# SwiGLU feed-forward block: the order in which the first 512 rows of x are loaded, transposed and projected

## The chip, the cores and the metric

The kernel runs on one core of a Trainium2 chip. A core has a matrix engine (TensorE, here PE, whose weight loads are listed apart as PEld), a vector engine (VectorE, DVE), a scalar engine (ScalarE, ACT), GpSimd (POOL) and a sync engine (SyncE, SP); 16 DMA engines move data between the chip's memory and the core's on-chip memory (SBUF). Matmul results go to a small accumulator memory (PSUM). SP and ACT each have a queue on which they issue DMAs. The metric is the device time of one execution in microseconds.

## The reference

```python
B, S, D, F = 1, 2048, 640, 1536          # all in bfloat16
g = silu(x @ w_gate)                      # x [2048, 640], w_gate [640, 1536]
u = x @ w_up                              # w_up [640, 1536]
return (g * u) @ w_down                   # w_down [1536, 640]
```

## The kernel before, in words

The 2048 rows are worked in four blocks of 512 (`sb`). A block is four chunks of 128 rows. The contraction of the first two products runs over D = 640, five slices of 128 (`KD`); F = 1536 is twelve slices of 128 (`KF`, index `fc`).

For each block and each `fc`, `proj` makes five matmuls of 512 columns with the slices of `w_gate` as weights, into the PSUM tile `pg`, and five with `w_up`, into `pu` (line 134). ACT takes the Silu of `pg` (line 180), DVE multiplies it with `pu` into `aT` (line 181). After the twelve `fc` come the matmuls of the down projection (lines 189 and 213), whose results are copied and stored.

The matmuls need x transposed, with D across partitions (`xT`). For blocks 1 to 3 a transposing DMA brings it (line 97). For block 0 it would come too late, so its four chunks are loaded as they are into `x_sb`, TensorE transposes each with five 128x128 matmuls against an identity into a PSUM tile `pt` (line 125), and DVE or ACT copies `pt` into `xT` (line 130). The PSUM tiles `po_a` and `po_b`, two buffers each, serve for `pt`.

What sets the order at the front:

- Two queues, SP and ACT, take the first loads (lines 82 to 87): chunk 0 on SP and chunk 2 on ACT, then chunk 1 on SP and chunk 3 on ACT; then the first 128 columns of `w_gate`, three slices on SP and two on ACT, and the same of `w_up`. Then SP alone issues the rest: columns 128 to 384 of `w_gate` and of `w_up` (`W_CHUNKS[1]`), and the larger pieces after them (line 71), `w_down` (line 94), the transposing loads (line 97). ACT has a load of its function table and a Silu on one column (`silu_first`, line 89) after its four loads.
- Each engine works through its instructions in the order written. Loads get their completion semaphores from a set of eight in turn; a load that takes a semaphore for the second time is issued only when the load that used it last has landed. ACT's and SP's early loads alternate in this: in the kernel before, x takes four of the eight and the first columns of the weights the other four, so the first load of line 71 is the ninth and waits for chunk 2, and the next ones wait for chunks 0, 3 and 1.
- `keep_order` ties the instructions of TensorE and of ACT at the front to the order as written. `warm(n)` puts n matmuls of 128 columns on a tile of ones into TensorE's stream (line 103); nobody reads their result.
- TensorE's order is: 18 such matmuls, the transposes of chunk 0 and chunk 2, four more (`N_GAP`), the transposes of chunks 1 and 3, two more, then `proj_pair` twice: five matmuls (line 149) on chunks 0 and 2, 256 columns that lie in two groups of 128, and five on chunks 1 and 3; then `pu` with 512 columns, and so on.

Chunks 0 and 2 are copied by DVE, five slices at once. Of chunks 1 and 3 ACT copies the first two slices and DVE the other three.

Of the kernel before, what the change touches and what calls it, by code (L numbers as in the profile page):

```python
# [10 lines left out]
def _body(  # L11
# [8 lines left out]
    nc = tc.nc  # L20
    P = nc.NUM_PARTITIONS
# [11 lines left out]
    KD = D // P  # L33
    KF = F // P
    S_BLK = 512
# [1 line left out]
    SUB = S_BLK // P  # L37
    DA = 512
    Q = 32
    N_WARM, N_GAP = 18, 4  # L40
    W_CHUNKS = [(0, 1), (1, 3), (3, 6), (6, 9), (9, 12)]
    assert D % P == 0 and F % P == 0 and S % S_BLK == 0 and D > DA and SUB == 4

# [8 lines left out]
    x_sb = consts.tile([P, SUB, D], bf16)  # L52
    xT = consts.tile([P, KD, S], bf16)
    wg_sb = consts.tile([P, KD, F], bf16)
    wu_sb = consts.tile([P, KD, F], bf16)
# [5 lines left out]
    x_v = x2.rearrange("(c p) d -> p c d", p=P)  # L61
    xt_v = x2.rearrange("s (kd p) -> s kd p", p=P)
    wg_v = w_gate.rearrange("(kd p) f -> p kd f", p=P)
    wu_v = w_up.rearrange("(kd p) f -> p kd f", p=P)
    wd_v = w_down.rearrange("(kf p) d -> p kf d", p=P)

    def wslice(a, b):
        return slice(a * P, b * P)

    def load_w(eng, dst, src, a, b):  # L70
        eng.dma_start(out=dst[:, :, wslice(a, b)], in_=src[:, :, wslice(a, b)])

    def load_x(eng, c0, c1):
        eng.dma_start(out=x_sb[:, c0:c1, :], in_=x_v[:, c0:c1, :])

    ones = consts.tile([P, P], bf16)
    silu_first = consts.tile([P, 1], f32)
# [1 line left out]

    queues = (nc.sync, nc.scalar)  # L80
    halves = ((0, KD // 2 + 1), (KD // 2 + 1, KD))
    for c in (0, 1):
        for i, eng in enumerate(queues):
            load_x(eng, c + 2 * i, c + 2 * i + 1)
    for dst, src in ((wg_sb, wg_v), (wu_sb, wu_v)):
        for eng, (k0, k1) in zip(queues, halves):
            eng.dma_start(out=dst[:, k0:k1, wslice(0, 1)], in_=src[:, k0:k1, wslice(0, 1)])
    load_w(nc.sync, wg_sb, wg_v, *W_CHUNKS[1])
    nc.scalar.activation(silu_first[:], ones[:, 0:1], ACT.Silu)  # L89
    load_w(nc.sync, wu_sb, wu_v, *W_CHUNKS[1])  # L90
# [10 lines left out]
    def warm(n):  # L101
        for _ in range(n):
            nc.tensor.matmul(  # L103
                pw[:, 0:P], lhsT=ones[:], rhs=ones[:], start=True, stop=True
            )

    def keep_order(engine):

        traced = [i for i in nc.cur_bb.bb.instructions if i.engine == engine]
        for a, b in zip(traced, traced[1:]):  # L110
            tc.add_manual_dep(
                b,
                a.name,
                mybir.DependencyInfo(
                    mybir.DependencyClass.NoSync, mybir.DependencyReason.DATA
                ),
                reason="keep_order",
            )

    def transpose_chunk(c, parts):  # L120
        c_sl = slice(c * P, (c + 1) * P)
        for copy, tag, k0, k1 in parts:
            pt = psum.tile([P, k1 - k0, P], bf16, tag=tag, name="pt")
            for kd in range(k0, k1):
                nc.tensor.transpose(  # L125
                    out=pt[:, kd - k0, :],
                    in_=x_sb[:, c, kd * P : (kd + 1) * P],
                    identity=ident[:],
                )
            copy(out=xT[:, k0:k1, c_sl], in_=pt[:])  # L130

    def proj(ps, w_sb, fc, sb, c0, c1):
        for kd in range(KD):
            nc.tensor.matmul(  # L134
                ps[:, c0:c1],
                lhsT=w_sb[:, kd, fc * P : (fc + 1) * P],
                rhs=xT[:, kd, sb * S_BLK + c0 : sb * S_BLK + c1],
                start=(kd == 0),
                stop=(kd == KD - 1),
            )  # L140

    def proj_pair(ps, w_sb, fc, sb, b):


        def pair(ap):
            return ap.rearrange("p (a b c) -> p b a c", b=2, c=P)[:, b]

        for kd in range(KD):
            nc.tensor.matmul(  # L149
                pair(ps[:]),  # L150
                lhsT=w_sb[:, kd, fc * P : (fc + 1) * P],
                rhs=pair(xT[:, kd, sb * S_BLK : (sb + 1) * S_BLK]),
                start=(kd == 0),
                stop=(kd == KD - 1),
            )

    for sb in range(NSB):
        s_sl = slice(sb * S_BLK, (sb + 1) * S_BLK)
        for fc in range(KF):
            pg = psum.tile([P, S_BLK], f32, tag="gu", name="pg", bufs=4)  # L160
            pu = psum.tile([P, S_BLK], f32, tag="gu", name="pu", bufs=4)
            if sb == 0 and fc == 0:
                dve, act = nc.vector.tensor_copy, nc.scalar.copy
                warm(N_WARM)
                transpose_chunk(0, [(dve, "po_a", 0, KD)])
                transpose_chunk(2, [(dve, "po_b", 0, KD)])
                warm(N_GAP)
                for c in (1, 3):
                    transpose_chunk(c, [(act, "po_a", 0, 2), (dve, "po_b", 2, KD)])
                warm(2)  # L170
                proj_pair(pg, wg_sb, fc, sb, 0)
                proj_pair(pg, wg_sb, fc, sb, 1)
                proj(pu, wu_sb, fc, sb, 0, S_BLK)
                keep_order(mybir.EngineType.PE)
                keep_order(mybir.EngineType.Activation)
            else:
                proj(pg, wg_sb, fc, sb, 0, S_BLK)
                proj(pu, wu_sb, fc, sb, 0, S_BLK)
            sg = work.tile([P, S_BLK], f32)
            nc.scalar.activation(sg[:], pg[:], ACT.Silu)  # L180
            nc.vector.tensor_tensor(  # L181
                out=aT[:, fc, s_sl], in0=sg[:], in1=pu[:], op=ALU.mult
            )


        n_t = (SUB if sb < NSB - 1 else SUB - 1) * P
        po_t = psum.tile([P, n_t], f32, tag="po_b", name="po_t")
        for kf in range(KF):
            nc.tensor.matmul(  # L189
                po_t[:],  # L190
                lhsT=wd_sb[:, kf, DA:D],
                rhs=aT[:, kf, sb * S_BLK : sb * S_BLK + n_t],
                start=(kf == 0),
                stop=(kf == KF - 1),
            )
        ot_t = outp.tile([P, n_t], bf16, name="ot_t")
        ot_q = outp.tile([P, n_t], bf16, name="ot_q")
        nc.scalar.copy(ot_t[:], po_t[:])  # L198
        nc.vector.transpose(out=ot_q[:], in_=ot_t[:])  # L199
        for q in range(P // Q):  # L200
            nc.scalar.dma_start(
                out=out2[
                    sb * S_BLK : sb * S_BLK + n_t, DA + q * Q : DA + (q + 1) * Q
                ].rearrange("(i r) c -> r i c", r=Q),
                in_=ot_q[q * Q : (q + 1) * Q, :].rearrange("r (i c) -> r i c", c=Q),
            )

        for j in range(SUB):
            s0 = sb * S_BLK + j * P
            last = sb == NSB - 1 and j == SUB - 1  # L210
            po_a = psum.tile([P, DA], f32, tag="po_a", name="po_a")
            for kf in range(KF):
                nc.tensor.matmul(  # L213
                    po_a[:],
                    lhsT=aT[:, kf, s0 : s0 + P],
                    rhs=wd_sb[:, kf, 0:DA],
                    start=(kf == 0),
                    stop=(kf == KF - 1),
                )
            ot = outp.tile([P, DA], bf16, name="ot")  # L220
            nc.scalar.copy(ot[:], po_a[:])  # L221
            nc.sync.dma_start(out=out2[s0 : s0 + P, 0:DA], in_=ot[:])
            if last:
                po_b = psum.tile([P, D - DA], f32, tag="po_b", name="po_b")
                for kf in range(KF):
                    nc.tensor.matmul(  # L226
                        po_b[:],
                        lhsT=aT[:, kf, s0 : s0 + P],
                        rhs=wd_sb[:, kf, DA:D],
                        start=(kf == 0),  # L230
                        stop=(kf == KF - 1),
                    )
                ot_b = outp.tile([P, D - DA], bf16, name="ot_b")
                nc.vector.tensor_copy(out=ot_b[:], in_=po_b[:])  # L234
                nc.scalar.dma_start(out=out2[s0 : s0 + P, DA:D], in_=ot_b[:])
# [76 lines left out]
def kernel(tc, *args):  # L312
    _body(tc, *args)
    tc.close()
    tc.compile()
    _trim(tc.nc)
# [30 lines left out]
```

## Time and profile before

| what | value |
|---|---|
| median of six runs | 164.5 us (164.08 to 164.87) |
| the profiled execution's own time | 164.87 us |
| its span in the profile | 163.6 us |
| TensorE busy | 160.0 us, 98% of the span |
| weight loads (PEld) busy | 76.2 us, 47% |
| DVE busy | 37.8 us, 23% |
| ACT busy | 42.5 us, 26% |
| granted TensorE clock | 1.00 of full |

All times inside the profile count from the start of the span, which is SP's first DMA issue. In the timeline a line gives the start, the time, the engine, the line of the kernel, the operation, the tiles it writes and reads, and how many were merged; in brackets stands how long the engine had been idle before and what ended it. SPq and ACTq are the DMA issues on the queues of SP and ACT. In the list of DMA issues, the last number is the time from the issue to the landing. A matmul's record overlaps with the next one's, so the distance of their starts is the pace, not their duration.

### The profile page before, as it was taken

The numbers are of one execution on the slowest core, as the hardware profiler recorded it, in microseconds if no ns is written. First come the engines' busy times: TensorE is split into PE (matmuls) and PEld (weight loads), VectorE is DVE, ScalarE is ACT, GpSimd is POOL, SyncE is SP. The second block draws the span as 40 slices with busy tenths as digits, with TensorE's granted clock in tenths as the row PEclk, the third lists the DMA queues.
The fourth block names the chain that finished last, engine by engine and source line by source line (L and its number), as shares of the span: only waits on it lengthen the run. The fifth ranks groups of instructions, "written<-read, shape, count | busy, mean of one in ns | idle before, by whom it ended". The sixth has DMA issues, their size and how long they took to land.

```text
span 163.6 us, 1869 instructions
## 1 busy us (share of the span) xinstructions
PE 160.0 (98%) x766; PEld 76.2 (47%) x781; DVE 37.8 (23%) x58; ACT 42.5 (26%) x72; POOL 0.6 (0%) x6
## 2 busy tenths in 40 slices
PE   8999999999999999999999999999999999999994
PEld 7744444444444444444444444444444444445442
DVE  1233333310013333311003333331001333332000
ACT  3322222212142222212222222221214222222121
POOL 1000000000000000000000000000000000000000
DMA  7999999914100000003110000000420000000312
GB/s 217 272 334 329 364 125 220 204 23 68 64 32 0 0 0 0 4 0 34 64 64 0 2 4 0 0 0 0 64 68 32 0 0 0 0 0 4 53 35 72
DMA packets 26888, 11.26 MB, mean 69 GB/s; under 512 B 17664, under 2 KB 26880, under 8 KB 26880
## 3 DMA queue, kind: packets, MB, share of 16 engines
q1 hardware_dynamic: 17968, 10.16, 24.2%
q10 hardware_dynamic: 8912, 0.98, 3.9%
q8 instruction: 6, 0.10, 0.2%
q14 instruction: 2, 0.02, 0.0%
HBM read 6.55 MB, written 2.62 MB: 56 GB/s over the span
## 4 chain that ended last, share of the span: by engine, by line
PE 97%; DMA 2%; issue 1%; DVE 0%
PE pu L134 31%; PE pg L134 31%; PE po_a L213 25%; PE po_t L189 6%; DMA x_sb<-in_x_dram 2%; PE pt L125 1%; PE pg L149 1%; PE po_b L226 0%; PE pw L103 0%; DVE ot_b L234 0%
## 5 line engine op out<-in xcount | busy, mean ns | idle before, releaser
L134 PE MATMUL pu<-xT,wu_sb 128*128 128x512 bf16 x230 | 59.0, 379 | 0.5
L134 PE MATMUL pg<-xT,wg_sb 128*128 128x512 bf16 x235 | 58.4, 379 | 0.0
L181 DVE TENSOR_TENSOR aT<-sg,pu 128x512 bf16<-128x512 f32 x48 | 33.0, 687 | 100.9 <-PE pu L134 100.9
L180 ACT ACTIVATE sg<-pg 128x512 f32<-128x512 f32 x48 | 28.7, 597 | 71.6 <-PE pg L134 70.1
L213 PE MATMUL po_a<-wd_sb,aT 128*128 128x512 bf16 x188 | 41.9, 379 | 0.2
L134 PEld LDWEIGHTS <-wu_sb 128*128 128x128 bf16 x240 | 23.4, 98 | 28.2 <-DMA wu_sb<-in_w_up_dram 0.4
L134 PEld LDWEIGHTS <-wg_sb 128*128 128x128 bf16 x235 | 22.9, 98 | 27.9 <-DMA wg_sb<-in_w_gate_dram 0.4
L213 PEld LDWEIGHTS <-aT 128*128 128x128 bf16 x192 | 18.8, 98 | 22.6
L221 ACT CAST ot<-po_a 128x512 bf16<-128x512 f32 x16 | 9.4, 585 | 32.4 <-PE po_a L213 19.3
L189 PE MATMUL po_t<-aT,wd_sb 128*128 128x512 bf16 (+1 forms) x47 | 10.3, 365 | 0.1
L189 PEld LDWEIGHTS <-wd_sb 128*128 128x128 bf16 x48 | 4.7, 98 | 5.1
L198 ACT CAST ot_t<-po_t 128x512 bf16<-128x512 f32 (+1 forms) x4 | 2.2, 559 | 11.6 <-PE po_t L189 11.6
L199 DVE STREAM_TRANSPOSE ot_q<-ot_t 128x512 bf16<-128x512 bf16 (+1 forms) x4 | 2.7, 678 | 9.1 <-ACT ot_t L198 9.1
L103 PE MATMUL pw<-ones 128*128 128x128 bf16 x24 | 3.2, 313 | 0.4 <-DVE ones L78 0.4
L103 PEld LDWEIGHTS <-ones 128*128 128x128 bf16 x24 | 2.6, 148 | 0.4 <-DVE ones L78 0.4
L125 PE MATMUL pt<-ident,x_sb 128*128 128x128 bf16 x20 | 2.5, 313 | 0.2 <-DMA x_sb<-in_x_dram 0.2
L234 DVE CAST ot_b<-po_b 128x128 bf16<-128x128 f32 x1 | 0.3, 291 | 9.9 <-PE po_b L226 9.9
L130 DVE COPY xT<-pt 128x640 bf16<-128x640 bf16 (+1 forms) x4 | 1.7, 424 | 3.8 <-PE pt L125 3.8
L125 PEld LDWEIGHTS <-x_sb 128*128 128x128 bf16 x20 | 2.1, 147 | 0.5 <-DMA x_sb<-in_x_dram 0.5
L89 ACT ACT_TABLE_LOAD x1 | 1.3, 1283 | 2.0 <-issue 2.0
L149 PE MATMUL pg<-xT,wg_sb 128*128 128x256 bf16 x10 | 1.5, 310 | 0.0
L149 PEld LDWEIGHTS <-wg_sb 128*128 128x128 bf16 x10 | 1.1, 119 | 0.2
(11 smaller groups left out, 3.6 us busy)
## 6 DMA issues: line engine op xcount, KB each, us to landing
out_dram<-ot SPq DMA_DIRECT2D x16, 128.0 KB, 1.7
wd_sb<-in_w_down_dram SPq DMA_DIRECT2D x1, 1920.0 KB, 12.9
wg_sb<-in_w_gate_dram SPq DMA_DIRECT2D x3, 480.0 KB, 7.7
wu_sb<-in_w_up_dram SPq DMA_DIRECT2D x3, 480.0 KB, 7.5
out_dram<-ot_q ACTq DMA_DIRECT2D x12, 32.0 KB, 1.9
x_sb<-in_x_dram SPq DMA_DIRECT2D x2, 160.0 KB, 2.9
x_sb<-in_x_dram ACTq DMA_DIRECT2D x2, 160.0 KB, 3.3
wg_sb<-in_w_gate_dram SPq DMA_DIRECT2D x1, 320.0 KB, 4.8
```

The source lines that it names most:

```text
L103: nc.tensor.matmul(pw[:, 0:P], lhsT=ones[:], rhs=ones[:], start=True, stop=True)
L125: nc.tensor.transpose(out=pt[:, kd - k0, :], in_=x_sb[:, c, kd * P : (kd + 1) * P], identity=ident[:],)
L130: copy(out=xT[:, k0:k1, c_sl], in_=pt[:])
L134: nc.tensor.matmul(ps[:, c0:c1], lhsT=w_sb[:, kd, fc * P : (fc + 1) * P], rhs=xT[:, kd, sb * S_BLK + c0 : sb * S_BLK + c1], start=(kd == 0 ...
L149: nc.tensor.matmul(pair(ps[:]), lhsT=w_sb[:, kd, fc * P : (fc + 1) * P], rhs=pair(xT[:, kd, sb * S_BLK : (sb + 1) * S_BLK]), start=(kd == ...
L180: nc.scalar.activation(sg[:], pg[:], ACT.Silu)
L181: nc.vector.tensor_tensor(out=aT[:, fc, s_sl], in0=sg[:], in1=pu[:], op=ALU.mult)
L189: nc.tensor.matmul(po_t[:], lhsT=wd_sb[:, kf, DA:D], rhs=aT[:, kf, sb * S_BLK : sb * S_BLK + n_t], start=(kf == 0), stop=(kf == KF - 1),)
L198: nc.scalar.copy(ot_t[:], po_t[:])
L199: nc.vector.transpose(out=ot_q[:], in_=ot_t[:])
L213: nc.tensor.matmul(po_a[:], lhsT=aT[:, kf, s0 : s0 + P], rhs=wd_sb[:, kf, 0:DA], start=(kf == 0), stop=(kf == KF - 1),)
L221: nc.scalar.copy(ot[:], po_a[:])
```

## The change

Chunks 0 and 1 are each loaded in two halves of 64 rows, one half on each queue; after them chunk 2 goes on SP and chunk 3 on ACT. That makes three x loads on each queue in place of two. The loads of the weights follow in the same order as before. With two loads more ahead of line 71, the semaphores are met one load earlier on each queue: the first loads of `w_up` take those of the two halves of chunk 0, the first two loads of line 71 those of the halves of chunk 1, and the next two those of chunks 3 and 2.

TensorE transposes the chunks in the order 0, 1, 2, 3, with three fillers in place of four between the second and the third. Chunk 2's copy becomes one DVE copy of five slices; chunk 3's stays shared by ACT and DVE. The first gate projection works on columns 0 to 256 and then on 256 to 512, which are now contiguous, so `proj_pair` goes. The tiles `po_a` and `po_b` of the transposes are shared out anew.

```diff
-    N_WARM, N_GAP = 18, 4
+    N_WARM, N_GAP = 18, 3
...
-    def load_x(eng, c0, c1):
-        eng.dma_start(out=x_sb[:, c0:c1, :], in_=x_v[:, c0:c1, :])
+    def load_x(eng, c, p0, p1):
+        eng.dma_start(out=x_sb[p0:p1, c, :], in_=x_v[p0:p1, c, :])
...
+    def load_halves(dst, src, a, b):
+        for eng, (k0, k1) in zip(queues, halves):
+            eng.dma_start(out=dst[:, k0:k1, wslice(a, b)], in_=src[:, k0:k1, wslice(a, b)])
+
     for c in (0, 1):
         for i, eng in enumerate(queues):
-            load_x(eng, c + 2 * i, c + 2 * i + 1)
-    for dst, src in ((wg_sb, wg_v), (wu_sb, wu_v)):
-        for eng, (k0, k1) in zip(queues, halves):
-            eng.dma_start(out=dst[:, k0:k1, wslice(0, 1)], in_=src[:, k0:k1, wslice(0, 1)])
+            load_x(eng, c, i * P // 2, (i + 1) * P // 2)
+    for i, eng in enumerate(queues):
+        load_x(eng, 2 + i, 0, P)
+    load_halves(wg_sb, wg_v, *W_CHUNKS[0])
+    load_halves(wu_sb, wu_v, *W_CHUNKS[0])
...
                 transpose_chunk(0, [(dve, "po_a", 0, KD)])
-                transpose_chunk(2, [(dve, "po_b", 0, KD)])
+                transpose_chunk(1, [(dve, "po_b", 0, KD)])
                 warm(N_GAP)
-                for c in (1, 3):
-                    transpose_chunk(c, [(act, "po_a", 0, 2), (dve, "po_b", 2, KD)])
+                transpose_chunk(2, [(dve, "po_a", 0, KD)])
+                transpose_chunk(3, [(act, "po_b", 0, 2), (dve, "po_a", 2, KD)])
                 warm(2)
-                proj_pair(pg, wg_sb, fc, sb, 0)
-                proj_pair(pg, wg_sb, fc, sb, 1)
+                proj(pg, wg_sb, fc, sb, 0, 2 * P)
+                proj(pg, wg_sb, fc, sb, 2 * P, S_BLK)
                 proj(pu, wu_sb, fc, sb, 0, S_BLK)
```

More of the change, by code (lines that the diff above doesn't have):

```diff
@@ L140, in proj @@
             )
[L142 to L155, printed above, removed]
     for sb in range(NSB):
```

## The prediction

> **What bounds the kernel now.** The page comes first: how much of the span is tensor work, and what the chain that ended last is made of.
>
> ```profile
> span 163.6 us, 1869 instructions
> ...
> PE 97%; DMA 2%; issue 1%; DVE 0%
> ```
>
> TensorE is the chain nearly from end to end; nothing in the steady part is changed, so the edit can move only the 2% of DMA and the 1% of issue at the front. The chain cut to the first 12 us shows where these lie.
>
> ```profile
> 0.00 2.67 DMA x_sb<-in_x_dram
> 2.67 0.05 issue
> 2.71 1.25 PE pt L125 x10
> 3.96 0.43 PE pw L103 x4
> 4.38 1.07 PE pt L125 x10
> 5.45 0.21 PE pw L103 x2
> 5.67 1.33 PE pg L149 x10
> 7.00 0.05 issue
> 7.05 1.03 PE pu L134 x4
> ```
>
> The first load of x lands at 2.67, and from then on TensorE is never without work: ten transposes, four fillers, ten transposes, two fillers, the first gate projection. That picture suggests that an earlier first chunk is worth its full gain. The timeline of all engines says otherwise:
>
> ```profile
> 0.40 2.10 PE L103 MATMUL pw<-ones 128*128 128x128 bf16 x18 [0.40 <-DVE ones L78]
> ...
> 2.05 1.28 ACT L89 ACT_TABLE_LOAD   x1 [2.05 <-issue]
> 2.71 0.98 PEld L125 LDWEIGHTS <-x_sb 128*128 128x128 bf16 x10 [0.48 <-DMA x_sb<-in_x_dram]
> ...
> 3.08 0.37 SPq L71 DMA_DIRECT2D wg_sb<-in_w_gate_dram  x1
> ...
> 7.96 0.76 PEld L134 LDWEIGHTS <-wg_sb 128*128 128x128 bf16 x5 [0.38 <-DMA wg_sb<-in_w_gate_dram]
> ...
> 9.07 0.76 PEld L134 LDWEIGHTS <-wu_sb 128*128 128x128 bf16 x5 [0.35 <-DMA wu_sb<-in_w_up_dram]
> ```
>
> A weight load (PEld) waits at 7.96 for the second chunk of w_gate and at 9.07 for that of w_up. Both come just as TensorE needs them: the pu block before (five at the 0.215 us pace of the later blocks, the first missing from the records) began at about 6.84 and was through at 7.91, so TensorE itself lost some 0.05 us. After 9.08 the blocks follow every 1.08 us without a wait. So the end is set by the later of two things: TensorE's own work up to 7.91, and the arrival of these two loads. The list of DMA issues gives their price:
>
> ```profile
> wg_sb<-in_w_gate_dram SPq DMA_DIRECT2D x1, 320.0 KB, 4.8
> wu_sb<-in_w_up_dram SPq DMA_DIRECT2D x1, 320.0 KB, 5.5
> ```
>
> 3.08 + 4.8 = 7.9 and 3.49 + 5.5 = 9.0. SP issues the first as late as 3.08 because it waits: 1.2 us, by the waits of SP, for a load of x. The loads take turns on eight completion semaphores, and the ninth load must see its semaphore's first load, x chunk 2 on ACT (issued 0.12, landed 2.9 later), come in.
>
> **Change, part by part.** (Landing = issue + time to landing, from the x tile's own view: SP's loads 2.7 and 3.0 us, ACT's 2.9 and 3.6, issued at 0.00, 0.45, 0.12 and 0.57.) The four chunks landed at about 2.67 (chunk 0), 3.02 (2), 3.5 (1) and 4.13 (3), one after the other.
>
> *Chunk 0 in halves.* Bytes and order stay: first 160 KB, then 160 KB, and so on, over the same 16 engines. What could come earlier is the ramp: in 1.0 to 1.6 us only 60 packets moved, at 128 GB/s, all on SP's queue; in 1.6 to 2.4 it was 346 GB/s with both. Bounds for the start of the first transpose, now 2.71: down to 2.29, the end of the 18 fillers (last start 2.18 plus 0.107), and up by 0.22, if the first half of chunk 1 slips in ahead of ACT's half (80 KB at the 359 GB/s of the stretch 2.4 to 3.2). *Chunk 1 next.* It takes the place that chunk 2 had, 3.02; transposes of a chunk take 5 x 0.107 = 0.53. Second block: before 3.24, now no earlier than 3.02. So at most 0.22 of the 0.42 survives.
>
> The Trainium skill ("DMA: Bandwidth & Descriptors", Rules for kernel authors) speaks against this edit: of two transfers to disjoint partition halves it says "Don't bother — they serialize", since both use the same engines. By that rule the first transpose stays at 2.71, and the filler alone would be saved. The one-queue ramp speaks a little for the edit, and no row here decides.
>
> *N_GAP 4 to 3.* One filler, 0.107 us, leaves TensorE's stream. *Chunks 2 and 3.* Wanted at 3.02 + 0.53 + 0.32 = 3.87 and 4.41 at the earliest; they have the third and fourth places, 3.5 and 4.13, so nothing waits. TensorE's own stream thus becomes 0.11 to 0.33 us shorter (longer by 0.11 in the bad case); I take 0.2, between.
>
> *Copies.* Chunk 2's copy is one on DVE (0.49) where ACT (0.37) and DVE (0.36) shared it. A copy starts 0.75 after its chunk's first transpose (2.71 to 3.46): chunk 3's last ends by 4.41 + 0.75 + 0.36 = 5.52; the second half of the projection, which reads it, comes five matmuls of 0.21 after 5.13, at 6.2. Covered by 0.7. *Projection.* Ten 128x256 matmuls remain; their pace, 0.21 and later 0.109, is half of that of 512 columns, so the strided pairing cost nothing that could be saved.
>
> *One more DMA on each queue* (0.43 us each on SP by the gate load's row, 0.46 on ACT). The first w_gate loads move from 0.91 to about 1.36 and from 1.04 to 1.5. They landed at 4.75 and 4.98; at worst 0.45 later, 5.2, against a need at 5.46 - 0.33 = 5.13: at most 0.07, and likelier nothing, since their bytes stand behind all of x, 640 KB, which at these rates moves until 3.2 or so.
>
> *New wait.* There are ten loads before the big ones, for eight semaphores: the first w_up load on each queue now waits for its half of chunk 0. Queued behind it on ACT: table load and the warm Silu, 2.02 us from that issue to their end (1.53 to 3.55); with chunk 0 at 2.29 to 2.67 they end at 4.31 to 4.69, before ACT's copy is wanted (0.45 after its chunk's first transpose, as 4.63 after 4.18, so 4.86 and later). Cover 0.2, then another 0.7 of the copy's own. On SP: w_up's issue (0.49), then the second w_gate chunk, which also waits for ACT's half of chunk 1. So it goes out at the later of 2.67 + 0.49 + 0.05 = 3.2 and 3.02 + 0.06 = 3.08. Bounds: 2.83 (chunk 0 at 2.29, chunk 1 at chunk 0's old 2.67) and 3.5 (ACT's half of chunk 1 takes 2.9 from its issue at 0.57): 0.25 earlier to 0.42 later than 3.08. I take 3.14, 0.06 later, between the two nearest. First w_up itself: 2.67 + 4.0 = 6.67 at worst, needed at 6.5 to 6.7; not counted.
>
> *Sum.* TensorE reaches its need of w_gate at 7.91 - 0.2 = 7.7; the load lands at 7.9 + 0.06. The load decides: the gain turns into a longer wait at 7.96, and the end moves by +0.06. The profiled execution took 164.87 (163.6 of span and 1.27 around it), so 164.93; it stands 0.37 above the median of the runs, 164.5, so on their scale about 164.6. A change of 0.3%, 0.5 us, is about what a measurement of this kernel can tell.
>
> The trace has one more thing that could spoil the sum. The granted clock reads 1.00 throughout, yet the first three 128x256 matmuls take 421 to 348 ns and those from 6.07 on 272: the pace doubles there. The skill ("TensorE: Matmul & The Clock Gate", Part 1) says that this follows about 3.4 us of activity, counted by a window that does not start with the kernel. By that page the step may move between runs; an estimate from it, 1 us later, would cost 0.5 us, of which the longer wait would now absorb 0.2.
>
> **Rivals.**
> *The weights do not bind (faster).* If in most executions they land 0.3 us earlier than in this profile, TensorE's own stream counts in full: 0.33 at the best ordering, with the 0.05 stall 0.38; should chunk 1 come early too, 0.42 + 0.11 + 0.05 = 0.58. Time 163.9 to 164.2. For it: the profiled execution is the slowest of those shown (164.08 to 164.87). Against: both 0.38 and 0.35 waits stand in it.
> *The weight stream slips by a whole issue (slower).* One DMA more per queue delays the second w_gate and w_up chunks by 0.42 to 0.49: 165.0. Place: SP before the line 71 loads; it decides as soon as they go out after 3.2. For it: the rate of the DMA dips to 147 GB/s in 4.4 to 5.2, just where these loads start, so what is issued later is not caught up. Against: SP idled 1.2 us there.
> *ACT late (slower).* The table load behind a late chunk 0 would have to slip by 0.9 us before TensorE waits; at 3.2 instead of 2.67, it costs nothing yet. Price past that one for one, 0.3: 164.9.
> *Halving does nothing.* Chunk 0 lands at 2.67 as before: TensorE gains only 0.11, and the weights decide as in the forecast: 164.6.
>
> **How the numbers follow.** Weights decide, with or without an earlier chunk 0: 0.55 (within 0.3% 0.46, slower 0.06, faster 0.03). Weights not binding: 0.18 (faster 0.14, the rest within). Whole issue: 0.22 (slower 0.17). ACT: 0.05, slower. So faster 0.17, same 0.55, slower 0.28. Range: the likeliest case from 0.25 earlier to 0.42 later is 164.25 to 164.9; the rivals take it to 163.9 and 165.2 (0.49 on top of up to 0.2 of drift between medians).
>
> **What would show it.** Right: the wait of the weight load for w_gate before about 7.96 grows from 0.38 to 0.5 or more while the first transpose or the projection is earlier; the line 71 loads go out between 3.0 and 3.3; SP's and ACT's first w_up issue stand behind chunk 0's landing. Wrong: no wait for w_gate and a block at 9.08 moved earlier (first rival), line 71 at 3.4 or later (second), or TensorE waiting for xT.

## The result and the profile after

The changed kernel is slower: 166.03 us in the median of 21 runs (164.81 to 166.91) against 164.48 in 45 runs of before (163.87 to 164.89), a ratio of 1.0090 with an interval of 1.0075 to 1.0105. In two later sets of runs it took 165.58 against 164.24 (1.0072, 1.0036 to 1.0108) and 165.38 against 164.43 (1.0066, 1.0038 to 1.0094). Not only the median rose: the runs of before lie within 1.0 us, those of the changed kernel within 2.1. One more run of it, at 167.61, lies over 1.5% above its fastest; it counts as slow and is left out.

The profiled execution of the changed kernel took 165.41, near the low end of its runs, while that of before, 164.87, stood at the high end of its own. So these two profiles show only 0.5 us of the 1.5. First the page of the changed kernel:

```profile
span 164.1 us, 1870 instructions
...
PE 96%; DMA 2%; issue 1%; ACTq 0%; DVE 0%
```

The chain of the first 12 us (start, length, what) says where the 0.5 us came in. The second half of chunk 1, issued by ACT at 0.70, now stands in it in place of chunk 0:

```profile
0.12 0.54 ACTq L74
0.66 0.04 issue
0.70 3.04 DMA x_sb<-in_x_dram
3.73 0.05 issue
3.78 0.71 PE pt L131 x5
4.49 0.32 PE pw L109 x3
4.81 1.07 PE pt L131 x10
```

The timeline of the changed kernel, with the idle time before an instruction and what ended it in brackets:

```profile
0.00 1.83 SPq L74 DMA_DIRECT2D x_sb<-in_x_dram  x3
0.12 2.00 ACTq L74 DMA_DIRECT2D x_sb<-in_x_dram  x3
...
2.68 0.45 PEld L131 LDWEIGHTS <-x_sb 128*128 128x128 bf16 x5 [0.46 <-DMA x_sb<-in_x_dram]
...
3.75 0.37 SPq L71 DMA_DIRECT2D wg_sb<-in_w_gate_dram  x1
3.77 0.45 PEld L131 LDWEIGHTS <-x_sb 128*128 128x128 bf16 x5 [0.64 <-DMA x_sb<-in_x_dram]
...
5.89 1.76 PE L140 MATMUL pg<-xT,wg_sb 128*128 128x256 bf16 x10
...
8.34 0.96 PEld L140 LDWEIGHTS <-wg_sb 128*128 128x128 bf16 x5
```

Chunk 0 is used at 2.68, as before (2.71). Then TensorE pauses a second time, until it can use chunk 1 at 3.77 (the second half landed at 3.73); before, the second block of transposes followed the first without a pause. The weight load at 8.34 has no bracket: the wait for w_gate, on which the forecast rested, is gone. TensorE itself is late.

The x tile's own view gives the cost of an issue (least, median, most, in ns). Before:

```profile
L74 SPq DMA_DIRECT2D x_sb<-in_x_dram x2: 394/404/415, 0.0 to 0.5; - x2
L74 ACTq DMA_DIRECT2D x_sb<-in_x_dram x2: 415/432/449, 0.1 to 0.6; - x2
```

And the changed kernel:

```profile
L74 SPq DMA_DIRECT2D x_sb<-in_x_dram x3: 571/574/589, 0.0 to 1.2; - x3
L74 ACTq DMA_DIRECT2D x_sb<-in_x_dram x3: 542/602/787, 0.1 to 1.5; - x3
```

Half the bytes took longer to issue, 0.54 to 0.79 us in place of 0.39 to 0.45, and the whole chunks 2 and 3 behind them, with 0.59 and 0.60, too. The table by stage shows the DMA over the same time (the last two columns are the share of the 16 engines and GB/s). Before:

```profile
1.00:1.60 0.60, 0.60 (x9) 0.60 (x7) 0.00 (x0) 0.00 (x0) 0.00 (x0) 1.00 0.77 128
1.60:2.40 0.80, 0.80 (x9) 0.63 (x6) 0.00 (x0) 0.35 (x1) 0.00 (x0) 1.00 1.02 346
2.40:3.20 0.80, 0.58 (x6) 0.49 (x6) 0.00 (x0) 0.80 (x1) 0.00 (x0) 1.00 1.03 359
```

The changed kernel:

```profile
1.00:1.60 0.60, 0.60 (x8) 0.60 (x7) 0.00 (x0) 0.00 (x0) 0.00 (x0) 1.00 0.30 70
1.60:2.40 0.80, 0.80 (x9) 0.62 (x6) 0.00 (x0) 0.00 (x0) 0.00 (x0) 1.00 0.82 224
2.40:3.20 0.80, 0.60 (x6) 0.45 (x5) 0.00 (x0) 0.04 (x1) 0.00 (x0) 1.00 0.97 256
```

By 3.2 us that makes 0.6 x 128 + 0.8 x 346 + 0.8 x 359 = 641 KB before and 426 KB after: 215 KB behind, 0.6 us at 359 GB/s. The first packet of x moves at 1.35 us in place of 1.02. That is 0.33 later, while the first issue is only 0.18 longer, so the longer issue alone does not account for the delay.

From the first 512-column block of `pu` of the second `fc` on (9.08 before, 9.64 after), both kernels take the same 154.5 us to the end of the span. In all profiles below this rest is 154.4 to 154.5 us, so everything is decided ahead of this block.

### The profile page after: what moved, and what is told of

Read it like the earlier page. It is cut to its first block, busy times and chain, and to the rows that moved or that the text cites. A ratio compares the mean times of both kernels' runs of the same rounds, so it can differ in the third digit from the quotient of the medians.

```text
span 164.1 us, 1870 instructions
## 1 busy us (share of the span) xinstructions
PE 160.2 (98%) x765; PEld 76.3 (46%) x780; DVE 38.0 (23%) x58; ACT 42.1 (26%) x71; POOL 0.6 (0%) x6
## 4 chain that ended last, share of the span: by engine, by line
PE 96%; DMA 2%; issue 1%; ACTq 0%; DVE 0%
PE pg L140 32%; PE pu L140 31%; PE po_a L204 25%; PE po_t L180 6%; DMA x_sb<-in_x_dram 2%; PE pt L131 1%; PE po_b L217 0%; ACTq L74 0%; PE pw L109 0%; DVE ot_b L225 0%
## 5 line engine op out<-in xcount | busy, mean ns | idle before, releaser
L140 PE MATMUL pg<-xT,wg_sb 128*128 128x512 bf16 (+1 forms) x245 | 60.1, 377 | 0.0
L204 PEld LDWEIGHTS <-aT 128*128 128x128 bf16 x192 | 18.8, 98 | 22.5
L217 PEld LDWEIGHTS <-aT 128*128 128x128 bf16 x12 | 0.8, 98 | 0.2
L217 PE MATMUL po_b<-wd_sb,aT 128*128 128x128 bf16 x12 | 0.8, 219 | 0.0
```

The source lines that it names most:

```text
L140: nc.tensor.matmul(ps[:, c0:c1], lhsT=w_sb[:, kd, fc * P : (fc + 1) * P], rhs=xT[:, kd, sb * S_BLK + c0 : sb * S_BLK + c1], start=(kd == 0 ...
L204: nc.tensor.matmul(po_a[:], lhsT=aT[:, kf, s0 : s0 + P], rhs=wd_sb[:, kf, 0:DA], start=(kf == 0), stop=(kf == KF - 1),)
L217: nc.tensor.matmul(po_b[:], lhsT=aT[:, kf, s0 : s0 + P], rhs=wd_sb[:, kf, DA:D], start=(kf == 0), stop=(kf == KF - 1),)
```

## The experiments

Two theories stood at the start. A: the halved loads are slow to issue and feed the DMA late. B: TensorE's pauses put off the moment at which its pace doubles, which differs from run to run and so explains the spread. Theory C, the rival: the new order of chunks, the copies or the contiguous projection cost the time. For B the row to watch is the first projection: ten matmuls of 256 columns take 1.1 us at the fast pace (0.109 apart) and 2.1 at the slow one (0.213).

**The changed kernel again.** No edit.

> The changed kernel once more, for a second profile. Theory A (slow issue): SP's and ACT's six x issues of line 74 again take 0.54 to 0.79 us each, against 0.39 to 0.45 before, and the second half of chunk 1 lands at about 3.7. Theory B (pace): the moment from which the matmuls of 256 columns follow each other in 0.109 instead of 0.213 us moves from run to run (6.07 in the profile of before, about 6.9 in the first one of the change); a profiled execution at or above the median of 166.0 should show it later than 6.9, by about 2 us for each us of time. If the pace doubles at 6.9 again in an execution of 166 or more, B falls.

165.58 us (5 runs). The issues took 0.55 to 0.77 us on ACT and 0.57 to 0.59 on SP, and chunk 1 was in at 3.77: as A says. The pace doubled at 7.21, by the starts of single matmuls, against 6.93 in the first profile. That is the direction of B, though the execution was not as slow as the 166 at which B was to be put to the test. The timeline shows it as a longer projection:

```profile
5.93 1.88 PE L140 MATMUL pg<-xT,wg_sb 128*128 128x256 bf16 x10
```

**Whole chunks in the new order.**

```diff
-    for c in (0, 1):
+    for c in (0, 2):
         for i, eng in enumerate(queues):
-            load_x(eng, c, i * P // 2, (i + 1) * P // 2)
-    for i, eng in enumerate(queues):
-        load_x(eng, 2 + i, 0, P)
+            load_x(eng, c + i, 0, P)
```

> The changed kernel, but chunks 0 to 3 loaded whole, 0 and 2 on SP, 1 and 3 on ACT: two x loads on each queue and eight loads ahead of line 71, as in the kernel before. Only the order of chunks, the copies, the contiguous projection and the missing filler are left of the change. Theory A or B (the halved loads do it): back to 164.3 to 164.6, issues of 0.4 us, chunks landing at 2.7, 3.0, 3.5 and 4.1. Theory C (order, copies or projection do it): 165.5 to 166.

164.47 us, ratio 1.0006 (0.9982 to 1.0031): no difference to before. Issues were back at 0.40 to 0.44:

```profile
L74 SPq DMA_DIRECT2D x_sb<-in_x_dram x2: 398/406/415, 0.0 to 0.5; - x2
L74 ACTq DMA_DIRECT2D x_sb<-in_x_dram x2: 398/420/443, 0.1 to 0.6; - x2
```

Theory C falls: the interval leaves it 0.3% at most. Chunks 2 and 3 landed late in this profile, at 4.37 and 4.62, and made one pause of 0.74 us; that did not show in the median.

**The halves in the old order.** In the kernel before:

```diff
-    def load_x(eng, c0, c1):
-        eng.dma_start(out=x_sb[:, c0:c1, :], in_=x_v[:, c0:c1, :])
+    def load_x(eng, c, p0, p1):
+        eng.dma_start(out=x_sb[p0:p1, c, :], in_=x_v[p0:p1, c, :])
...
-    for c in (0, 1):
+    for c in (0, 2):
         for i, eng in enumerate(queues):
-            load_x(eng, c + 2 * i, c + 2 * i + 1)
+            load_x(eng, c, i * P // 2, (i + 1) * P // 2)
+    for i, eng in enumerate(queues):
+        load_x(eng, 1 + 2 * i, 0, P)
```

> The kernel before with the change's loads alone: chunk 0 and chunk 2, which it transposes second, come in two 64-row halves on both queues, then chunks 1 and 3 whole; TensorE's order, four fillers, copies and paired projection stay. Theory A or B: 165.5 to 166.1, second block of transposes at about 3.8. Theory C: 164.3 to 164.6.

165.16 us, 1.0059 (1.0034 to 1.0084). The loads alone bring most of the loss, if somewhat less than the 165.5 expected. TensorE paused twice, for 0.33 and 0.53 us; the second block of transposes began at 3.65, not at 3.8:

```profile
3.65 0.71 PE L127 MATMUL pt<-ident,x_sb 128*128 128x128 bf16 x5 [0.33 <-DMA x_sb<-in_x_dram]
```

Both runs together put the loss on the halves.

**Both pauses filled.**

```diff
-    N_WARM, N_GAP = 18, 3
+    N_WARM, N_GAP = 22, 3
...
+                warm(5)
                 transpose_chunk(1, [(dve, "po_b", 0, KD)])
```

> The changed kernel with TensorE's two early pauses filled: 22 fillers in place of 18 at the start and 5 more between the transposes of chunks 0 and 1 (0.43 and 0.53 us of fillers, about the pauses before 2.69 and 3.78). The loads are the same. Theory B: what the late doubling of the pace costs goes away, 164.9 to 165.3, and the spread of the runs narrows to about 0.8 us. Theory A without B: nothing gained, 166.0 to 166.3.

164.70 us (164.31 to 165.12), 1.0026 (1.0006 to 1.0045). With the same loads, nine more matmuls that nobody reads won 0.88 us against the 165.58 of the same chip, and the spread fell to 0.8 us. The transposes of chunk 1 begin at 3.78 with the fillers as without them, so nothing came earlier; what is won is pace. In the timeline the projection runs at the fast pace, and the weights arrive just in time. The brackets are idle time of the weight loads; the matmuls themselves follow each other without a gap:

```profile
5.72 1.26 PE L140 MATMUL pg<-xT,wg_sb 128*128 128x256 bf16 x10
...
7.88 0.76 PEld L140 LDWEIGHTS <-wg_sb 128*128 128x128 bf16 x5 [0.32 <-DMA wg_sb<-in_w_gate_dram]
...
8.94 0.78 PEld L140 LDWEIGHTS <-wu_sb 128*128 128x128 bf16 x5 [0.30 <-DMA wu_sb<-in_w_up_dram]
```

**Fewer fillers in the kernel before.**

```diff
-    N_WARM, N_GAP = 18, 4
+    N_WARM, N_GAP = 12, 4
```

> The kernel before with 12 fillers in place of 18 at the start, and nothing else: its loads, and so everything that TensorE waits for, are those of before. TensorE's pause before the first transpose grows from 0.42 to about 1.06 us, about the sum of the two pauses in the changed kernel; the fillers' results are read by nobody. Theory B (pauses put off the doubling of the pace): median 164.8 to 165.6 with single runs up to 166 or more, and in a slow profile the pace doubles after 6.1. Against B: 164.2 to 164.5, nothing changes, since no wait has moved.

164.34 us, 1.0011 (0.9990 to 1.0031): nothing. B in its first form, that any pause of about 1 us delays the pace, falls. The pause in this profile was 0.83 us, and the pace doubled at 4.47 in spite of it.

**Halves by columns.**

```diff
-    def load_x(eng, c, p0, p1):
-        eng.dma_start(out=x_sb[p0:p1, c, :], in_=x_v[p0:p1, c, :])
+    def load_x(eng, c, d0, d1):
+        eng.dma_start(out=x_sb[:, c, d0:d1], in_=x_v[:, c, d0:d1])
...
-            load_x(eng, c, i * P // 2, (i + 1) * P // 2)
+            load_x(eng, c, i * D // 2, (i + 1) * D // 2)
...
-        load_x(eng, 2 + i, 0, P)
+        load_x(eng, 2 + i, 0, D)
```

> The changed kernel, but chunks 0 and 1 are halved by columns: 128 rows of 320 columns on each queue in place of 64 rows of 640. As many loads, bytes and semaphore waits as in the changed kernel. If the 64-row form is what makes the issues slow: issues of 0.40 to 0.45 us, chunk 1 in by about 3.1, median 164.3 to 165.0. If any third load on each queue does it: issues stay at 0.54 to 0.79 or the chunks land as late as 3.7, median 165.5 to 166.0.

166.46 us, but in only four runs (164.97 to 166.94), 1.0109 (1.0052 to 1.0166). Half of the expectation came: it is the 64-row form that makes issues slow, for 128 rows of 320 columns took the old time (the x tile's view):

```profile
L74 SPq DMA_DIRECT2D x_sb<-in_x_dram x3: 397/410/432, 0.0 to 0.9; - x3
L74 ACTq DMA_DIRECT2D x_sb<-in_x_dram x3: 397/448/453, 0.1 to 1.0; - x3
```

Chunk 1 was in by 3.14, against 3.52 to 3.94 for the second chunk in the eight profiles with 64-row halves, and the first packet moved at 1.03, against 1.34 to 1.35 in those. So the 64-row form also starts the data later. But the time did not come back: the DMA fell to 130 GB/s between 2.4 and 3.2,

```profile
2.40:3.20 0.80, 0.80 (x9) 0.60 (x8) 0.13 (x1) 0.49 (x1) 0.00 (x0) 1.00 0.68 130
```

and chunks 2 and 3 took 4.2 and 4.3 us from issue to landing, so the pause only moved and grew. A short issue alone does not mend the change. Why the DMA fell is open; chunk 2, issued at 0.45 in the two kernels with whole chunks in the new order, landed at 4.37 in one profile and at 3.28 in the other, so part of it may be chance. The timeline of this run is the clearest case of a late pace:

```profile
5.17 1.25 PE L131 MATMUL pt<-ident,x_sb 128*128 128x128 bf16 x10 [1.17 <-DMA x_sb<-in_x_dram]
...
6.42 2.34 PE L140 MATMUL pg<-xT,wg_sb 128*128 128x256 bf16 x10
...
8.98 1.20 PE L140 MATMUL pu<-xT,wu_sb 128*128 128x512 bf16 x4 [0.22 <-issue]
```

All ten matmuls ran at 0.213; the pace doubled only at 9.37.

**More fillers in the kernel before.**

```diff
-    N_WARM, N_GAP = 18, 4
+    N_WARM, N_GAP = 22, 4
```

> The kernel before with 22 fillers in place of 18, which just fill its pause before the first transpose. Theory B: the pace doubles earlier or as early, TensorE comes to its need of w_gate sooner, and the median is 0 to 0.3 us lower (163.9 to 164.3), held by the arrival of the weights. Against B: 0 to 0.2 us slower, where a chunk 0 that lands early has to wait for the fillers.

164.38 us, 1.0009 (0.9992 to 1.0027): no gain. The kernel before loses nothing by its one pause.

**Whole chunks in the new order, pauses filled.** The loads of the second run, and:

```diff
-    N_WARM, N_GAP = 18, 3
+    N_WARM, N_GAP = 22, 4
```

> The changed kernel with its chunks loaded whole (0 and 2 on SP, 1 and 3 on ACT) and 22 and 4 fillers in place of 18 and 3: the new order without halves and nearly without pauses. Theory A with B: 164.0 to 164.4, no worse than before. Theory C (the order costs): 164.7 or more.

164.18 us, 1.0006 (0.9987 to 1.0024), as before. With whole chunks nothing of the loss is left, and the new order wins nothing either.

**No early work at all.** In the kernel before:

```diff
-    N_WARM, N_GAP = 18, 4
+    N_WARM, N_GAP = 0, 4
```

> The kernel before without the 18 fillers at the start; loads and all waits are those of before. The run with 12 fillers had a pause of 0.83 us and lost nothing, so theory B is narrowed: the pace doubles at the end of a stretch of some 3 to 4 us in which TensorE was busy for more than about three quarters, and the stretches do not start with the kernel; a single short pause passes, two pauses of 1.0 us together often do not. Without any early work the first such stretch can only begin at the first transpose, 2.5 to 2.7. Narrowed B: the pace doubles no earlier than 5.9 and up to 9, median 164.9 to 165.5, single runs to 166. Against B (the pace has nothing to do with the end): 164.1 to 164.5.

164.88 us (164.06 to 165.87), 1.0041 (1.0013 to 1.0070). Leaving out matmuls that nobody reads, before a wait that stays, makes the kernel 0.6 us slower. That is what theory B says, with the loads untouched. The link to the pace rests here on the times alone, since the profiled execution, 164.58, lies below the median and shows no late doubling. In this profile the pace doubled at 5.74, a little earlier than the 5.9 expected, since chunk 0 landed at 2.08:

```profile
2.12 1.25 PE L125 MATMUL pt<-ident,x_sb 128*128 128x128 bf16 x10 [2.12 <-DMA x_sb<-in_x_dram]
...
5.12 1.55 PE L149 MATMUL pg<-xT,wg_sb 128*128 128x256 bf16 x10
```

**One pause filled, then the other.** First only the second, with `warm(5)` before the transposes of chunk 1:

> The changed kernel with five fillers between the transposes of chunks 0 and 1 alone; the first pause, of 0.4 us, stays. Narrowed B: one pause of 0.4 us is what the kernel before has too, so nearly all of the gain of filling both comes back: 164.7 to 165.0. If each pause costs its share: about half way, 165.2 to 165.5.

Then only the first, with 22 fillers in place of 18:

> The changed kernel with 22 fillers in place of 18 alone; the second pause, of 0.6 to 0.75 us, stays. Narrowed B: one pause below 0.85 us, so 164.7 to 165.1, as the kernel with both filled (164.7) and at most a little more. If each pause costs its share: 165.2 to 165.5; if only the second counts: 165.6 or more.

164.68 us, 1.0023 (1.0011 to 1.0035), and 164.88, 1.0035 (1.0019 to 1.0050, five runs). Filling either one brings nearly all that filling both brought (164.70); the shares do not add, so the two pauses act together. That their plain sum decides is not shown: two pauses of 0.86 us together (the halves in the old order) went with a loss of 0.59%, one pause of 0.83 (fewer fillers) with none that could be measured.

With only the second pause filled the pace doubled at 5.09, and then another wait shows. The first columns of `w_gate`, issued at 1.88 and 2.15 in place of 0.91 and 1.04, landed at 5.78 and 5.57 in place of 4.75 and 4.98, and TensorE's row stood still for 0.33 us (the bracket is shorter, because a matmul's record outlasts its place in the row):

```profile
5.82 1.27 PE L140 MATMUL pg<-xT,wg_sb 128*128 128x256 bf16 x10 [0.16 <-DMA wg_sb<-in_w_gate_dram]
```

**Fewer loads ahead.** In the changed kernel with both pauses filled (22 fillers and `warm(5)`):

```diff
-    load_halves(wg_sb, wg_v, *W_CHUNKS[0])
-    load_halves(wu_sb, wu_v, *W_CHUNKS[0])
+    load_w(nc.sync, wg_sb, wg_v, *W_CHUNKS[0])
+    load_w(nc.scalar, wu_sb, wu_v, *W_CHUNKS[0])
```

> The changed kernel with both pauses filled (as in the run that took 164.7) and only eight loads ahead of the big ones: the first columns of w_gate come in one load on SP and those of w_up in one on ACT, so no first load of w_up waits for chunk 0 any more, and the second w_gate chunk waits for ACT's half of chunk 0 in place of chunk 1 and can go out near 2.6 in place of 3.68. If the later weights are what is left of the loss against before: 164.2 to 164.4, and the waits for w_gate and w_up near 7.9 and 8.9 are shorter or earlier. If not: 164.6 to 164.8.

165.05 us in four runs, 1.0052 (1.0036 to 1.0069): a miss, slower. The line 71 loads went out at 2.66 as meant, but the undivided first columns of w_gate landed at 5.76, and TensorE waited for them:

```profile
5.81 0.99 PEld L140 LDWEIGHTS <-wg_sb 128*128 128x128 bf16 x10 [0.68 <-DMA wg_sb<-in_w_gate_dram]
```

The edit replaced one wait by another and decided nothing. So the late loads were put into the kernel before, alone, by splitting the first columns of w_up:

```diff
-    N_WARM, N_GAP = 18, 4
+    N_WARM, N_GAP = 22, 4
...
-    for dst, src in ((wg_sb, wg_v), (wu_sb, wu_v)):
-        for eng, (k0, k1) in zip(queues, halves):
+    first = [
+        (wg_sb, wg_v, ((0, 3), (3, 5))),
+        (wu_sb, wu_v, ((0, 2), (3, 4))),
+        (wu_sb, wu_v, ((2, 3), (4, 5))),
+    ]
+    for dst, src, parts in first:
+        for eng, (k0, k1) in zip(queues, parts):
```

> The kernel before with 22 fillers (0.0 to 0.2 us from before in its run), and the first columns of w_up in two loads on each queue in place of one. x and the first w_gate columns are issued as before; but there are ten loads ahead of line 71, as in the changed kernel, so that its first load waits for the second x load on ACT (chunk 3, in at 3.8 to 4.1) and goes out near 4.0 in place of 2.9 to 3.1. If late line 71 loads are what is left of the loss: 0.4 to 0.9 us slower than before, 164.6 to 165.1, with waits for w_gate and w_up after 8. If they are not: within 0.2 us of before.

164.52 us, 1.0015 (0.9997 to 1.0032): a miss again, and an answer. Line 71 went out at 3.81, later than in the changed kernel, yet w_gate was in at 7.24, no later than in the kernels that issued it at 2.9 (7.0 to 7.25). TensorE waited for it only because the pace had doubled very early here, at 3.89:

```profile
3.81 0.37 SPq L71 DMA_DIRECT2D wg_sb<-in_w_gate_dram  x1
...
7.28 0.76 PEld L139 LDWEIGHTS <-wg_sb 128*128 128x128 bf16 x5 [0.59 <-DMA wg_sb<-in_w_gate_dram]
```

The ten loads on eight semaphores, the wait that the forecast took for the change's main risk, cost at most 0.3%, and likelier nothing. What is left of the loss with the pauses filled, 0.46 us, comes with the halved loads, for whole chunks with filled pauses leave none of it. Part of it may be the fillers that stand in for the late chunk (four more than with whole chunks), part the wait for the first columns of `w_gate` above. That it comes by the 0.6 us that the DMA is behind at 3.2 fits, but was not tried by itself.

**The changed kernel a third time.**

> The changed kernel a third time. Two pauses again, of about 0.4 and 0.6 to 0.75 us; narrowed theory B: the pace doubles between 5.7 and 9.1, and the time follows it by half a us per us; 165.3 to 166.3.

165.38 us (164.47 to 166.48). The profiled execution took 165.93, and its pace doubled at 7.76:

```profile
6.10 2.05 PE L140 MATMUL pg<-xT,wg_sb 128*128 128x256 bf16 x10
```

The three profiles of the changed kernel side by side, with two others. A pause is counted from 0.107 us after the last matmul's start to the next one's start:

| kernel | TensorE's pauses, us | pace doubles at | execution, us |
|---|---|---|---|
| changed, first | 0.41 + 0.59 | 6.93 | 165.41 |
| changed, again | 0.29 + 0.75 | 7.21 | 165.58 |
| changed, third | 0.40 + 0.80 | 7.76 | 165.93 |
| changed, both filled | none | 5.49 | 164.76 |
| column halves | 0.15 + 1.37 | 9.37 | 166.87 |

From the first profile to the third, a doubling 0.83 us later and 0.20 us more of pauses go with 0.52 us more of time. This can be estimated from the paces above. Work before the doubling takes about twice its later time, so for the same work the time should follow half the sum of the doubling's moment and the pauses. The three profiles of the changed kernel and that of the column halves have the same work on TensorE. Half the sum is 3.97, 4.13, 4.48 and 5.45 us, and the execution time less this half is 161.43 to 161.46 in all four. The pauses and the late doubling together account for these differences to 0.03 us.

## Why the prediction was wrong

It foresaw 164.6 us, within 0.3% of before, and a range to 165.2; the median was 166.03.

- **"One more DMA on each queue."** This is the first step that failed. The half loads were priced like whole ones, 0.43 and 0.46 us; all six x issues took 0.54 to 0.79. The first w_gate load went out at 1.88, not at 1.36, and the first w_gate columns were in at 5.20 and 5.49, past the worst case of 5.2; TensorE, late itself, did not wait for them. For chunk 1 the price is small: ACT's half of it went out at 0.70 in place of 0.57.
- **"Chunk 0 in halves."** Held: the first transpose began at 2.69, within 2.29 to 2.93 and almost where it was. The Trainium skill's sentence on halves of a transfer ("DMA: Bandwidth & Descriptors", Rules for kernel authors) was right that nothing is won; the cost is what the runs added.
- **"Chunk 1 next. It takes the place that chunk 2 had, 3.02."** Failed: 3.73, beyond even the far bound of 3.5 for ACT's half, and this made the second pause, 0.59 us in the first profile. Against the 0.57 + 2.9 of that bound the half went out 0.13 us later and took 0.14 longer to land. The step took it that order and bytes fix the arrival, whatever the form of the load; the DMA was fed at 70 and 224 GB/s, not 128 and 346. So TensorE's own stream got longer (the first projection at 5.89 for 5.46), where the sum had it 0.2 shorter.
- **"The load decides."** It did not: w_gate landed at 8.13, later than the 7.96 of the forecast, and TensorE still came to it without a wait. Besides, the landing at 7.9 was taken from one profile. In five later profiles with whole loads, line 71 going out at 2.6 to 2.9, w_gate was in at 7.0 to 7.25, and in none of the five did a matmul wait for it. So the wait that was to swallow a change of TensorE's stream was mostly not there. That was the first rival's condition; its sign was wrong, since TensorE became later and not earlier. With pauses filled, weights and TensorE are close again, as the forecast had them.
- **The new wait.** Line 71 went out at 3.75, past the bound of 3.5, but a later issue alone costs nothing measurable (the run with the late weights). The second rival had the right sign and named the right queue, but the wrong price and path.
- **The step of the pace.** This is the term that was missing from the sum. The forecast named it, priced 1 us of delay at 0.5 us and then left it out of the sum without a reason. In the first profile the doubling came at 6.93 for 6.07. The two pauses together move it, at some 0.9 us of time: 165.58 to 164.70 when filled. The Trainium skill's rule ("TensorE: Matmul & The Clock Gate", Part 1: half rate until about 3.4 us of sustained activity, in a window that runs freely) agrees with the runs: the earliest doubling came 3.5 us after the first matmul (3.89 against 0.40), that of the kernel without early work 3.6 after it (5.74 against 2.12), and it moves between runs of one kernel. The granted clock reads 1.00 through all of it.
- **Copies, projection, order.** Held: whole chunks in the new order take the time of before, and in the changed kernel's profiles TensorE never waited for `xT`. (The copy that went from ACT and DVE to DVE alone is chunk 1's; chunk 2's was DVE's alone before.)

## What to carry to other kernels

A pause of TensorE in the first microseconds has two prices: its length, and a later doubling of the pace, which can be the larger one and shows in the spread of the runs and the length of one fixed block rather than in any wait. Before a load is split, look at what its issue costs in the new form and when its last part lands, since half the bytes may take longer to issue, and a short issue alone need not help; and where two engines' arrivals are nearly tied, one profile does not tell which of them decides.

## What the runs showed of the hardware

- A load of 64 rows by 1280 bytes took 0.54 to 0.79 us to issue, and the 128-row loads behind it on the queue took 0.59 and 0.60; 128 rows by 640 bytes, the same bytes, took 0.40 to 0.45. The first packet moved at 1.34 to 1.35 us in the eight profiles with 64-row loads and at 1.01 to 1.03 in the eight without. The reason is open.
- The pace of TensorE tolerated one pause of 0.4 to 0.83 us without a change in the median. Two pauses of 0.86 and of 1.0 us together went with losses of 0.6% and of 0.7 to 0.9%, of which filling won back the larger part in the second kernel; an idle start of 2.1 us went with 0.4%. Where the limit lies, and whether it is one of the sum or of the place, was not measured.
- The same load at the same place can land 1 us apart in two executions (chunk 2 at 3.28 and at 4.37).
